# Lightweight convolution and a two-layer silu block on Trainium2: the first blocks' taps in PSUM, an earlier halo, and a new order of the steady block

## The chip, the cores and the metric

The kernel runs on one core of one Trainium2 chip. The metric is the device time of one execution in microseconds (us). A core has five engines that run side by side, each with its own stream of instructions: PE (TensorE, matrix products), DVE (VectorE), ACT (ScalarE), POOL (GpSimd) and SP (SyncE, which here issues most DMA transfers). Matrix products land in PSUM, eight banks of 128 partitions by 512 numbers; everything else lies in SBUF. Instructions wait for each other through semaphores.

## The reference

```python
def _attn_ref(x, weight):                       # x 8 x 4096 x 192, weight 8 x 7
    w = softmax(weight, axis=-1)                # over the 7 taps of each head
    x_pad = concat([zeros(8, 6, 192), x], axis=1)
    out[b, s, c] = sum_i w[c // 24, i] * x_pad[b, s + i, c]
...
def _moe_ref(x, w_in, w_out):                   # x 32768 x 192, 192 x 2048, 2048 x 192
    h = x @ w_in
    g = h * (1.0 / (1.0 + np.exp(-h)))
    return (g @ w_out).astype(np.float32)
```

So each channel is smoothed over seven positions in time (with six zeros ahead of each of the 8 sequences), then each of the 32768 tokens goes up from 192 to 2048 numbers, through silu, and down to 192. Everything is fp32.

## The kernel before

**Blocks.** The tokens are cut into 32 blocks of 1024. A block has two halves of 512 tokens, one in partitions 0 to 63 and one in 64 to 127, and the 192 channels are three thirds of 64. Block b goes through these stages; the letters are the tokens by which the order names them.

- `ld` loads the block (SP, L156) into a buffer `nat`. `i` turns it over with VectorE's 32x32 transposes (L490) into `xt`, channels in partitions. `ha` (halo_in, L502) puts the last six columns of the block before into the first six columns of `xt`: a copy from a small tile `tail` (on ScalarE, L509, for the blocks 1 and 2, on GpSimd, L511, for later ones; at the start of a sequence GpSimd writes zeros), then an SP DMA for the other half (L512).
- `v.ki` (conv, L515) is tap i of third k. Tap 0 is a scaled copy by ScalarE into `nat` (L521). Taps 1 to 6 have two forms. For blocks 1 and 2 VectorE multiplies and adds in one instruction (L529, `nat<-xt,taps,nat`). For later blocks ScalarE writes a scaled copy to a buffer u (L524), and a GpSimd DMA adds it into `nat` (L525, 18 per block).
- `sp` (spread) copies `nat` with SP DMAs (L546) into `dup`, where each half block has all its channels on either half of the partitions. `w.0` to `w.5` (win) are sums of parts of `dup` on VectorE (L563 and L566). w.0 and w.1 take `dup` in, w.2 to w.5 build on these.
- The up product is made in five groups g. A group has 15 products `Pr.g` (L658, TensorE, two run side by side on the two halves of the rows of the array) where the plain way has 18: the sums of inputs (w) and of weights allow it. `u`, `X`, `a`, `b` add up the results: u is a copy by ScalarE out of PSUM into a u buffer (L707), X, a and b are sums on VectorE (L701), and `S` is silu on ScalarE (L719). A small rest goes through plain products `L` (L675) and `SL`.
- `t1` to `t13` are sums of silu's results (L783, VectorE): t1 to t4 over 128x2048 numbers in parts `tC` and `tD` of 128x1024 each, the others whole.
- The down product has 20 products `Qr.j` for each of four j (L794, TensorE, two side by side on the two halves of the columns) in place of 24. `O`, `C`, `d` are copies out of PSUM by ScalarE (L829, L831), `m` are sums on VectorE (L842), `o` transposes (L850), `st` the stores by SP (L857).

P8.2 is thus product 8 of group 2, and Q4.3 out product 4 with j = 3.

**Weights.** In the first 170 us the weights are loaded, rounded, and their sums are made on GpSimd (`combine`, `combine_out` with its list OUT_SUMS; in the profile these stand at L138, with `ws`, `wr`, `wall` and `wx` as outputs). Block 0 takes the plain way meanwhile: plain up products, 48 down steps (the tokens `dp`), then copies `cp`, transposes `op` (L897) and stores `stp` (L906).

**The order is written by hand.** Every instruction is pinned to its place in the program, and each engine runs its own instructions in that order. `START` is a list of tokens that is run once, `PLAN` one that is run once for each b. A token's first character gives its block:

```python
    BACK = {"-": 1, "=": 2, "+": -1, "~": 3, "*": -2}
...
    for t in START.split():
        step(2, t)
    for b in range(1, NB + 4):
        for t in plan:
            step(b, t)
```

So in one pass of PLAN, `-P8.2` belongs to block b-1, `w.0` to block b, `+v.12` to block b+1, `*ld.0` to block b+2 and `=st.3` to block b-2; a token whose block does not exist, or that has been done, is passed over. In START a bare token is block 2, `-` block 1, `=` block 0 and `+` block 3. The assignments CHAIN_BANKS, XBANKS, PLAIN_BANKS and OUT_BANKS say which PSUM bank each result lies in.

Of the kernel before, what the change touches and what calls it, by code (L numbers as in the profile page):

```python
# [11 lines left out]
AF = mybir.ActivationFunctionType  # L12
ALU = mybir.AluOpType
# [4 lines left out]
def kernel(  # L18
# [24 lines left out]
    nc = tc.nc  # L43
# [3 lines left out]
    H, K = weight.shape  # L47
# [30 lines left out]


    PLAN = (  # L80
# [24 lines left out]
    )  # L105
    START = (
# [9 lines left out]
    )  # L116
    QUEUE = (0, 4, 1, 2, 3)
    CHAIN_BANKS = (
        (5, 7, 2, 5, 3),
        (4, 3, 1, 4, 6),  # L120
        (0, 6, 0, 6, 0),
    )
    XBANKS = {
        2: (1, 6, 3, 6, 0),
        4: (2, 1, 7, 0, 2),
    }
    PLAIN_BANKS = (7, 2, 0)
    OUT_BANKS = {"DX": 0, "DY": 2, "D2": 1, "D3": 4, "DC": 2}

    def pin(ins):  # L130
        return tc.keep_in_program_order(ins)
# [61 lines left out]
    for k in range(NK):  # L193
        rows_k = hot[SQ * k : SQ * k + SQ]
        for sign, base in ((1, 0), (-1, grp - 1)):
            pool.affine_select(
                out=rows_k,
# [8 lines left out]
    for e in range(2):  # L206
        half = one_hot[R * e : R * e + R].rearrange("p (a c) -> p a c", a=2)
        pool.affine_select(
            out=half,
# [133 lines left out]
    def combine(g, e):  # L343
# [40 lines left out]
        (("o", 1), ("o", 1), "+", ("o", 4)),  # L384
        (("o", 4), ("o", 4), "+", ("o", 10)),
        (("x", 1), ("o", 11), "+", ("o", 4)),
        (("x", 2), ("o", 5), "+", ("x", 1)),
        (("x", 1), ("o", 8), "-", ("x", 1)),
        (("x", 3), ("o", 0), "-", ("x", 1)),
        (("o", 10), ("o", 9), "-", ("o", 10)),  # L390
        (("o", 9), ("o", 9), "-", ("x", 3)),
        (("o", 4), ("o", 4), "n", ("o", 4)),
        (("o", 11), ("o", 11), "+", ("o", 9)),
        (("x", 4), ("o", 8), "-", ("o", 11)),
        (("o", 5), ("o", 5), "+", ("o", 8)),
        (("o", 3), ("o", 0), "+", ("o", 3)),
        (("o", 8), ("o", 1), "-", ("o", 8)),
        (("x", 7), ("o", 2), "+", ("x", 1)),
        (("o", 2), ("o", 2), "+", ("o", 8)),
        (("o", 0), ("o", 0), "+", ("o", 7)),  # L400
        (("x", 5), ("o", 6), "+", ("x", 4)),
        (("o", 6), ("o", 6), "-", ("o", 0)),
        (("x", 6), ("o", 3), "-", ("x", 4)),
        (("o", 7), ("o", 7), "n", ("o", 7)),
        (("o", 10), ("o", 11), "-", ("o", 10)),
        (("x", 0), ("x", 0), "n", ("x", 0)),
    )
    OUT_FORMS = {
# [88 lines left out]
    def tail_of(b):  # L497
        if (b + 1) * TT % S:
            tails[b + 1] = xpool.tile([R, NK, pad], F32, tag="tail", name="tail", bufs=2)
            pin(nc.sync.dma_start(out=tails[b + 1], in_=xts[b][R:P, :, TB : TB + pad]))  # L500

    def halo_in(b, _):  # L502
        xt = xts[b]
        if b * TT % S == 0:
            nc.gpsimd.memset(xt[0:R, :, 0:pad], 0.0)
        else:
            head = xt[0:R, :, 0:pad]
            if b <= 2:
                pin(nc.scalar.copy(head, tails.pop(b)))  # L509
            else:  # L510
                pin(nc.gpsimd.tensor_copy(head, tails.pop(b)))  # L511
        pin(nc.sync.dma_start(out=xt[R:P, :, 0:pad], in_=xt[0:R, :, TB : TB + pad]))  # L512
        tail_of(b)

    def conv(b, k, i):  # L515

        src = xts[b][:, k, i : i + TB]
        dst = nats[b][:, k, :, :].rearrange("p k c -> p (k c)")
        tap = taps[:, k, i : i + 1]
        if i == 0:  # L520
            pin(nc.scalar.activation(dst, src, AF.Copy, scale=tap))  # L521
        elif b > 2:
            z = free.pop(0)
            pin(nc.scalar.activation(z, src, AF.Copy, scale=tap))  # L524
            pin(nc.gpsimd.dma_start(out=dst, in_=z, accum_op=ALU.add))  # L525
            free.append(z)
        else:
            pin(
                nc.vector.scalar_tensor_tensor(  # L529
                    out=dst, in0=src, scalar=tap, in1=dst, op0=ALU.mult, op1=ALU.add  # L530
                )
            )

# [48 lines left out]
    def rows(t, e):  # L582
        return t[R * e : R * e + R]
# [29 lines left out]
    cmbs, banks = {}, []  # L613
# [24 lines left out]
    def plain_bank(b, i):  # L638
        return banks[PLAIN_BANKS[i]]

# [144 lines left out]
    def out_bank(node):  # L785
        name, e = OUT_HOME[node]
        return rows(banks[OUT_BANKS[name]], e)

# [15 lines left out]
    def mid(i):  # L804
        if not mids:
            cmb = xpool.tile([P, 4, TB], F32, tag="cmb", name="cmb")
            mids.extend(cmb[:, c, :] for c in range(4))
            mids.extend(xpool.tile([P, TB], F32, tag="yx", name="yx", bufs=2) for _ in range(2))
            mids.append(xpool.tile([P, TB], F32, tag="m4", name="m4"))
        return mids[i]  # L810
# [22 lines left out]
    def out_sum(b, i):  # L833
# [4 lines left out]
            lambda: (out_bank("Y"), rows(mid(2), 1)),  # L838
            lambda: (banks[OUT_BANKS["D3"]], mid(1)),
            lambda: (banks[OUT_BANKS["D2"]], mid(0)),  # L840
        )[i]()
# [162 lines left out]
    for j in (1, 2):  # L1004
        load_in(j, nc.sync)
    turn_in(0, 2)
    conv(0, 2, 0)
    for n in range(2):
        act.copy(dups[0][:, n, 0, :], by_pe[0][n])
    for i in range(1, K):  # L1010
        conv(0, 2, i)
    src = nats[0][:, 2, :, :].rearrange("p k c -> p (k c)")
# [87 lines left out]
```

## Time and profile before

| | us |
|---|---|
| time before, median of 3 runs (2344.7 to 2345.49) | 2345.25 |
| the profiled execution | 2346.1 |
| its span, first to last instruction | 2344.4 |
| its mean granted TensorE clock | 0.993 |
| first out products of block 1 | 167.04 |
| 30 periods from there, first out product to first out product | to 2294.64 |
| VectorE's taps, one instruction (L529) | 0.752 to 0.95 |
| a sum in SBUF (L563); with an operand in PSUM (L701) | 0.69; 0.68 to 0.70 |

The span cut in 40 equal slices, one digit a slice: TensorE's busy tenths, those of GpSimd, and the tenths of full speed at which TensorE's clock was granted.

```profile
PE   9879999999999999999999999999999999999997
...
POOL 5932222122222122222122222122221222221100
PEclk9989999999999999999999999999999999999999
```

The second and third slices (59 to 176 us) are where TensorE is less than full, and where GpSimd is busiest. In the lists below, a line of waits reads: engine, output and line, the engine, tile and line it waited for, then us in total, times, longest. A line of the timeline reads: start, length (both in us from the start of the span), engine, line, operation, output and inputs, partitions x elements, and how many instructions in a row (xN); in brackets the idle time before the first of them and what ended it. SPq and POOLq are the DMA issues of SP and GpSimd. PE shows an instruction of a row of like ones: where two products run side by side, each is counted.

### The profile page before, as it was taken

What the parts mean: (1) busy time and instruction counts of PE and PEld (TensorE: products, weight loads), DVE (VectorE), ACT (ScalarE), POOL (GpSimd) and SP (SyncE); (2) the same over time, 40 slices, a digit from 0 to 9 for tenths busy, and PEclk for the clock granted to TensorE, in tenths of its full rate; (3) what the DMA queues carried; (4) which work ended last, traced back from release to release, by engine and by line L of the source; (5) the groups of instructions that cost most, each with busy time, mean ns of one, the idle gap of its engine ahead of it and who ended that gap; (6) DMA issues with size and microseconds to landing.
All of it is one profiled execution on the core that took longest, in us unless ns stands there. A gap on an engine that the chain in (4) does not pass through costs nothing.

```text
span 2344.4 us, 31919 instructions
## 1 busy us (share of the span) xinstructions
PE 2304.3 (98%) x10622; PEld 994.2 (42%) x10622; DVE 2060.9 (88%) x2302; ACT 1562.5 (67%) x2835; POOL 552.8 (24%) x698
## 2 busy tenths in 40 slices
PE   9879999999999999999999999999999999999997
PEld 5234344444344443444443444443444444444433
DVE  8858899888889888899888998888998889998887
ACT  6266667776667766667766677766677766677643
POOL 5932222122222122222122222122221222221100
PEclk9989999999999999999999999999999999999999
DMA  7345667656666556676556676556676566665401
GB/s 164 67 74 90 116 114 126 107 100 101 115 115 119 102 101 113 109 122 115 98 99 115 111 124 111 102 96 118 116 124 106 100 101 115 115 119 94 75 13 18
DMA packets 526276, 242.66 MB, mean 104 GB/s; under 512 B 431840, under 2 KB 436960, under 8 KB 526112
## 3 DMA queue, kind: packets, MB, share of 16 engines
q0 software_dynamic: 75616, 138.45, 34.8%
q1 hardware_dynamic: 449440, 102.04, 24.8%
q8 instruction: 84, 1.38, 0.3%
q14 instruction: 80, 0.66, 0.1%
q10 hardware_dynamic: 1056, 0.13, 0.0%
HBM read 31.46 MB, written 25.17 MB: 24 GB/s over the span
## 4 chain that ended last, share of the span: by engine, by line
PE 92%; POOL 4%; DMA 1%; SPq 1%; DVE 1%; issue 1%; ACT 0%; DVEq 0%; POOLq 0%; ACTq 0%
PE ps L794 45%; PE ps L658 44%; PE ps L675 2%; POOL ws L138 2%; POOL wr L138 2%; DMA dup<-nat 1%; POOL wall L138 0%; DMA ws<-wr 0%; POOL wx L138 0%; DVE win L563 0%; DMA g<-in_moe_w_in_dram 0%; SPq L156 0%; SPq L546 0%; SPq L249 0%; SPq L254 0%
## 5 line engine op out<-in xcount | busy, mean ns | idle before, releaser
L525 POOL DMA_DIRECT2D nat<-u x522 | 444.6, 883 | 1604.5 <-ACT u L524 1090.1
L794 PE MATMUL ps<-g,wall 128*64 128x512 f32 x1984 | 774.3, 594 | 0.4 <-DVE g L701 0.4
L658 PE MATMUL ps<-win,wr 64*128 64x512 f32 x1550 | 674.2, 599 | 11.9 <-ACT u L707 8.7
L658 PE MATMUL ps<-win,ws 64*128 64x512 f32 x1550 | 604.5, 597 | 0.0
L707 ACT COPY u<-ps 128x512 f32<-128x512 f32 x775 | 445.1, 588 | 103.7 <-PE ps L658 97.7
L794 PE MATMUL ps<-g,wx 128*64 128x512 f32 x1240 | 424.8, 592 | 0.0
L658 PE MATMUL ps<-dup,wr 64*128 64x512 f32 x868 | 398.0, 592 | 0.1
L794 PE MATMUL ps<-t,wall 128*64 128x512 f32 x992 | 391.1, 595 | 0.0
L794 PEld LDWEIGHTS ps<-g,wall 128*64 128x64 f32 x1984 | 224.0, 137 | 347.2 <-issue 323.7
L524 ACT ACTIVATE u<-xt,taps 128x512 f32<-128x512 f32 x522 | 359.5, 722 | 1.4
L701 DVE TENSOR_TENSOR g<-u,ps 128x512 f32<-128x512 f32 x465 | 313.9, 680 | 38.6 <-PE ps L658 28.2
L658 PEld LDWEIGHTS ps<-win,wr 64*128 64x128 f32 x1550 | 258.8, 187 | 167.2 <-issue 100.2
L658 PEld LDWEIGHTS ps<-win,ws 64*128 64x128 f32 x1550 | 241.0, 187 | 192.4 <-issue 136.9
L658 PE MATMUL ps<-dup,ws 64*128 64x512 f32 x682 | 304.2, 595 | 14.4 <-DVE ps L701 14.4
L719 ACT ACTIVATE g<-ps 128x512 f32<-128x512 f32 x465 | 269.2, 603 | 70.5 <-PE ps L658 70.5
L719 ACT ACTIVATE g<-g 128x512 f32<-128x512 f32 x465 | 277.4, 634 | 42.8 <-DVE g L701 42.8
L783 DVE TENSOR_TENSOR t<-g 128x1024 f32<-128x1024 f32 (+1 forms) x217 | 292.2, 1369 | 4.2 <-ACT g L719 0.7
L794 PE MATMUL ps<-t,wx 128*64 128x512 f32 x744 | 288.1, 594 | 0.0
L701 DVE TENSOR_TENSOR ps<-u,ps 128x512 f32<-128x512 f32 x310 | 212.8, 695 | 52.6 <-PE ps L658 44.8
L794 PEld LDWEIGHTS ps<-g,wx 128*64 128x64 f32 x1240 | 130.5, 137 | 222.6 <-issue 222.3
L829 ACT COPY cmb<-ps 64x512 f32<-64x512 f32 x124 | 72.0, 581 | 213.5 <-PE ps L794 213.5
L783 DVE TENSOR_TENSOR t<-g,t 128x2048 f32<-128x2048 f32 x93 | 210.0, 2285 | 1.1
(99 smaller groups left out, 2397.8 us busy)
## 6 DMA issues: line engine op xcount, KB each, us to landing
nat<-u POOLq DMA_DIRECT2D x522, 256.0 KB, 4.0
dup<-nat SPq DMA_DIRECT2D x345, 128.0 KB, 2.4
nat<-in_x_dram SPq DMA_DIRECT2D x382, 64.0 KB, 3.7
out_dram<-yx SPq DMA_DIRECT2D x248, 64.0 KB, 2.0
out_dram<-cmb SPq DMA_DIRECT2D x124, 64.0 KB, 2.0
raw<-in_moe_w_out_dram SPq DMA_DIRECT2D x8, 384.0 KB, 4.1
g<-in_moe_w_in_dram SPq DMA_DIRECT2D x8, 192.0 KB, 5.8
ws<-wr POOLq DMA_DIRECT2D x8, 192.0 KB, 5.9
```

Source lines behind the costliest of these rows:

```text
L138: return lambda *args, **kw: pin(getattr(self.engine, name)(*args, **kw))
L524: pin(nc.scalar.activation(z, src, AF.Copy, scale=tap))
L525: pin(nc.gpsimd.dma_start(out=dst, in_=z, accum_op=ALU.add))
L658: nc.tensor.matmul(to[:, cols], raw(g, *LEFT[e][r], e), rhs[:, cols], start=first, stop=True, skip_group_check=True,)
L675: nc.tensor.matmul(plain_bank(b, n and 1 + e)[:, cols], rows(wr[j] if own == e else ws[j], e)[:, a, k, :], rows(dups[b], e)[:, SLOT[e][2 * ...
L701: pin(nc.vector.tensor_tensor(out_, u, v, op=op))
L707: pin(nc.scalar.copy(us[b, g, o][:, cols], t1[:, cols]))
L719: pin(nc.scalar.activation(h, src, AF.Silu))
L783: pin(engine.tensor_tensor(g_part(to, js), g_part(u, js), g_part(v, js), op=op))
L794: nc.tensor.matmul(out_bank(node), out_form(OUT_FORMS[r])[:, j, :], g_part(OPERAND[r], j), start=first, stop=True, skip_group_check=True,)
L829: pin(nc.scalar.copy(to(), out_bank(node)))
```

## The change

1. *Taps of blocks 1 and 2.* The partial sums of their taps are kept in three PSUM banks (one for each third) instead of `nat`; only the last tap of a third writes `nat`.
2. *Halo.* ScalarE instead of GpSimd copies the halo of block 3 also. Block 4 begins a sequence, so GpSimd's copies begin with block 5.
3. *START.* w.3, w.4 and w.5 of block 1 stand right behind w.2, ahead of most of block 2's taps; they stood behind all of these.
4. *t1.* Its two VectorE sums of 128x1024 (tC1, tD1) become one sum by GpSimd over 128x1536 (tA1) and one by VectorE over 128x512 (tB1).
5. *PLAN* has a new order throughout, with other PSUM banks. Twenty-five weight sums of OUT_SUMS are the same ones in another order.

The number of matrix products and their operands' sizes stay. The line numbers of the new kernel are 10 higher than those given here from L546 on down, up to 5 higher a little above.

```diff
+++ halo_in, conv
-            if b <= 2:
+            if b <= 3:
                 pin(nc.scalar.copy(head, tails.pop(b)))
...
+    CONV_BANKS = (2, 3, 4)
+    taken = {}
...
+        taken[b, k] = taken.get((b, k), 0) + 1
+        acc = banks[CONV_BANKS[k]] if b in (1, 2) else dst
         if i == 0:
-            pin(nc.scalar.activation(dst, src, AF.Copy, scale=tap))
+            pin(nc.scalar.activation(acc, src, AF.Copy, scale=tap))
...
                 nc.vector.scalar_tensor_tensor(
-                    out=dst, in0=src, scalar=tap, in1=dst, op0=ALU.mult, op1=ALU.add
+                    out=dst if taken[b, k] == K else acc,
+                    in0=src,
+                    scalar=tap,
+                    in1=acc,
+                    op0=ALU.mult,
+                    op1=ALU.add,
+++ START
-        "-w.0 -w.1 =dp.35 =dp.36 v.00 =dp.37 =dp.38 -w.2 =dp.39 =dp.40 =dp.41 v.01 =dp.42 v.20 "
-        "=dp.43 =dp.44 v.02 v.03 v.10 v.11 v.12 v.13 v.14 v.15 v.16 v.04 v.05 v.06 v.22 v.23 "
-        "v.24 v.25 v.26 =dp.45 =cp.0 =dp.46 =dp.47 =cp.1 v.21 -w.3 =cp.2 -w.4 -w.5 =op.0 =op.1 "
+        "-w.0 -w.1 =dp.35 =dp.36 v.00 =dp.37 =dp.38 -w.2 -w.3 -w.4 -w.5 =dp.39 =dp.40 =dp.41 "
+        "v.01 =dp.42 v.20 =dp.43 =dp.44 v.02 v.03 v.10 v.11 v.12 v.13 v.14 v.15 v.16 v.04 v.05 "
+        "v.06 v.22 v.23 v.24 v.25 v.26 =dp.45 =cp.0 =dp.46 =dp.47 =cp.1 v.21 =cp.2 =op.0 =op.1 "
+++ PLAN: its beginning, then the steps around the turn from up to out products
-        "=Q10.1 =Q7.2 =Q6.0 =Q10.2 =Q10.0 =Q8.2 =Q10.3 =Q8.0 -w.2 +i.0 =Q8.1 =Q1.1 =d.b =d.B "
-        "=Q1.2 =Q7.1 =Q8.3 -w.3 =Q2.2 -w.5 +i.2 =Q2.0 =m.1 =Q19.0 -X2.4 =m.0 +ha.0 =m.4 =Q2.3 "
-        "=Q7.0 -w.4 -P13.4 -u2.0 =m.5 =m.3 =m.2 -SL.0 +v.10 -P1.4 -P9.4 +v.20 -P1.0 -P5.1 "
...
-        "-P6.2 -b5.1 -X2.3 -u2.2 -S5.1 -b5.0 -P1.3 -a0.1 -P9.3 -X4.3 -P13.3 -P14.1 -P1.2 -S2.3 "
-        "-P3.2 -tD1 -u0.3 -P7.3 -P11.3 -u0.2 -P0.3 -P12.3 -S5.0 -X2.2 -S3.1 -P9.2 -P0.2 -a5.3 "
-        "-u1.3 -S4.3 -P13.2 -P4.3 -u1.2 -tC2 -X4.2 -P14.3 -P12.2 -b1.3 -P14.2 -P7.2 =o.2 -S2.2 "
-        "sp.0 -b1.2 -P11.2 -P10.3 -P10.2 -a1.3 P5.4 -a5.2 -S1.0 sp.2 -P8.3 -S0.1 +v.22 -tC3 "
-        "-S3.3 P5.0 -P4.2 -S4.2 -S3.2 -b5.2 +v.01 -b5.3 u5.4 +v.14 +v.26 -S5.2 -S5.3 L.00 "
-        "-Q17.0 -Q4.2 -Q17.2 -a0.3 u5.0 -Q4.1 -S1.1 -Q17.1 w.0 -Q4.0 w.1 -tD2 -a1.2 -Q4.3 "
-        "-Q17.3 P2.0 P3.4 -S0.3 -O.0 -tD3 -S1.3 P2.4 -C.0 -S1.2 -S0.0 u4.4 -P8.2 -tC4 -Q12.1 "
+        "=Q14.1 =t13 +i.2 =Q14.0 +i.0 =Q1.2 +ha.0 =Q19.0 -w.4 =Q1.0 =Q10.2 -u2.0 =Q19.3 =d.A "
+        "=Q8.3 =Q10.1 =Q8.2 =Q10.3 =Q7.1 =Q10.0 =Q7.3 =Q2.0 =Q8.0 =Q2.2 =Q2.3 =d.B =d.b -u2.4 "
+        "=m.4 =Q8.1 -X2.4 =m.3 -P3.0 -P1.0 -P1.4 =m.5 -X2.0 -P13.4 -P9.4 -P5.1 -u0.0 -P13.0 "
+        "-P0.0 =m.1 -S2.4 -u0.4 +v.20 -P0.4 =m.2 -P9.0 -P12.4 -X4.4 -u5.1 -S2.0 -P11.4 -u1.4 "
...
+        "-tB1 sp.1 -P8.0 -b5.0 -X4.1 -a0.0 -P2.2 -u1.1 -P12.1 -P3.3 -P6.3 -b1.1 -S1.4 -P11.1 "
+        "-tA1 -P7.1 -u2.3 -X2.3 -u4.2 -P10.1 -P14.1 -a5.1 -S4.1 -S5.0 -P6.2 -S3.1 -u2.2 -b5.1 "
+        "-P9.3 -X4.3 *ld.1 ~st.3 -P1.3 -P13.3 -P4.1 -P3.2 -S5.1 -u0.3 -P1.2 -S2.3 -u0.2 -X2.2 "
+        "-a1.1 -P7.3 -P11.3 -P12.3 -P0.3 +v.12 -P9.2 -a5.3 -tC2 -P0.2 -P13.2 -P4.3 -S4.3 +v.24 "
+        "-u1.3 -P8.1 -S2.2 -P14.3 -X4.2 -b1.3 -u1.2 -P7.2 -P14.2 -a0.1 -a5.2 -a1.3 -P12.2 "
+        "-P11.2 -P10.3 -S1.1 -b1.2 -S3.3 -P4.2 -P8.3 -S1.3 -S0.1 -b5.3 -P10.2 P5.4 sp.0 -S1.0 "
+        "-S3.2 sp.2 -a1.2 P5.0 -a0.3 -S5.3 -b5.2 -P8.2 -Q4.3 -S1.2 +v.04 -Q17.1 -Q17.3 -Q4.2 "
+        "-a0.2 +v.15 -S5.2 -S4.2 -Q4.1 u5.0 -Q17.2 -tC4 w.0 u5.4 -Q4.0 -Q17.0 -O.0 L.00 w.1 "
+        "-C.0 P2.4 -tC3 -tD2 P2.0 P3.4 +v.23 +v.02 u4.0 u4.4 -S0.2 -Q5.1 -Q16.3 -Q3.2 -Q16.0 "
...
+++ banks
-    CHAIN_BANKS = ((5, 7, 2, 5, 3), (4, 3, 1, 4, 6), (0, 6, 0, 6, 0))
+    CHAIN_BANKS = ((5, 4, 2, 3, 3), (7, 5, 0, 1, 6), (0, 6, 4, 7, 2))
-    XBANKS = {2: (1, 6, 3, 6, 0), 4: (2, 1, 7, 0, 2)}
+    XBANKS = {2: (1, 1, 4, 7, 0), 4: (1, 0, 6, 6, 0)}
-    PLAIN_BANKS = (7, 2, 0)
-    OUT_BANKS = {"DX": 0, "DY": 2, "D2": 1, "D3": 4, "DC": 2}
+    PLAIN_BANKS = (0, 0, 2)
+    OUT_BANKS = {"DX": 7, "DY": 2, "D2": 1, "D3": 4, "DC": 2}
```

Steps of `tA` and `tB` exist in the kernel before too, unused: tA is GpSimd over the first three of four quarters of a sum, tB VectorE over the last.

More of the change, by code (lines that the diff above doesn't have):

```diff
@@ L118 @@
     CHAIN_BANKS = (
-        (5, 7, 2, 5, 3),
-        (4, 3, 1, 4, 6),
-        (0, 6, 0, 6, 0),
+        (5, 4, 2, 3, 3),
+        (7, 5, 0, 1, 6),
+        (0, 6, 4, 7, 2),
     )
     XBANKS = {
-        2: (1, 6, 3, 6, 0),
-        4: (2, 1, 7, 0, 2),
-    }
-    PLAIN_BANKS = (7, 2, 0)
-    OUT_BANKS = {"DX": 0, "DY": 2, "D2": 1, "D3": 4, "DC": 2}
+        2: (1, 1, 4, 7, 0),
+        4: (1, 0, 6, 6, 0),
+    }
+    PLAIN_BANKS = (0, 0, 2)
+    OUT_BANKS = {"DX": 7, "DY": 2, "D2": 1, "D3": 4, "DC": 2}
     def pin(ins):
@@ L386 @@
         (("x", 1), ("o", 11), "+", ("o", 4)),
+        (("o", 4), ("o", 4), "n", ("o", 4)),
         (("x", 2), ("o", 5), "+", ("x", 1)),
@@ L391 @@
         (("o", 9), ("o", 9), "-", ("x", 3)),
-        (("o", 4), ("o", 4), "n", ("o", 4)),
         (("o", 11), ("o", 11), "+", ("o", 9)),
         (("x", 4), ("o", 8), "-", ("o", 11)),
-        (("o", 5), ("o", 5), "+", ("o", 8)),
         (("o", 3), ("o", 0), "+", ("o", 3)),
-        (("o", 8), ("o", 1), "-", ("o", 8)),
-        (("x", 7), ("o", 2), "+", ("x", 1)),
-        (("o", 2), ("o", 2), "+", ("o", 8)),
         (("o", 0), ("o", 0), "+", ("o", 7)),
@@ L402 @@
         (("o", 6), ("o", 6), "-", ("o", 0)),
-        (("x", 6), ("o", 3), "-", ("x", 4)),
+        (("o", 5), ("o", 5), "+", ("o", 8)),
+        (("x", 7), ("o", 2), "+", ("x", 1)),
+        (("o", 8), ("o", 1), "-", ("o", 8)),
+        (("o", 2), ("o", 2), "+", ("o", 8)),
         (("o", 7), ("o", 7), "n", ("o", 7)),
         (("o", 10), ("o", 11), "-", ("o", 10)),
+        (("x", 6), ("o", 3), "-", ("x", 4)),
         (("x", 0), ("x", 0), "n", ("x", 0)),
```

25 rows, old and new, of the table PLAN are left out of this document.

## The prediction

> **What bounds the kernel now.** First part 1 of the page, which gives busy time by engine, and the waits of TensorE.
>
> ```profile
> span 2344.4 us, 31919 instructions
> PE 2304.3 (98%) x10622; PEld 994.2 (42%) x10622; DVE 2060.9 (88%) x2302; ACT 1562.5 (67%) x2835; POOL 552.8 (24%) x698
> ```
>
> ```profile
> PE ps L658 <- DVE ps L701: 14.4, 1, 14.4
> PE ps L658 <- ACT u L707: 8.7, 3, 7.2
> ```
>
> TensorE bounds it, and its two long waits happen once each. The change leaves all 5311 matmuls in place (two records each), so it can only win time in which TensorE stands still or works unpaired. I therefore looked for that time stage by stage in the timeline: the start (up to 167.0, when the first out products run), 30 steady blocks (167.04 to 2294.64, mean period 70.92) and the tail.
>
> **The start.** The timeline by engine, around the two waits:
>
> ```profile
> 68.55 15.64 DVE L529 SCALAR_TENSOR_TENSOR nat<-xt,taps,nat 128x512 f32<-128x512 f32 x18
> ...
> 89.00 15.64 DVE L529 SCALAR_TENSOR_TENSOR nat<-xt,taps,nat 128x512 f32<-128x512 f32 x18
> ...
> 107.15 1.88 DVE L897 STREAM_TRANSPOSE osb<-cmb 128x512 f32<-128x512 f32 x3
> ...
> 120.90 1.30 DVE L490 STREAM_TRANSPOSE xt<-nat 128x512 f32<-128x512 f32 x2 [11.28 <-DMA nat<-in_x_dram]
> ...
> 122.12 0.67 DVE L701 TENSOR_TENSOR ps<-u,ps 128x512 f32<-128x512 f32 x1
> ...
> 107.87 6.70 SPq L906 DMA_DIRECT2D out_dram<-osb  x12
> ...
> 114.61 4.23 SPq L156 DMA_DIRECT2D nat<-in_x_dram  x8
> ...
> 131.29 0.20 POOL L511 COPY xt<-tail 64x18 f32<-64x18 f32 x1
> ...
> 131.52 1.95 ACT L521 ACTIVATE nat<-xt,taps 128x512 f32<-128x512 f32 x3 [22.03 <-POOL xt L511]
> ...
> 122.85 1.22 PE L658 MATMUL ps<-dup,ws 64*128 64x512 f32 x1 [14.45 <-DVE ps L701]
> ...
> 135.08 1.22 PE L658 MATMUL ps<-win,wr 64*128 64x512 f32 x1 [7.22 <-ACT u L707]
> ```
>
> The reader is to see two chains. The first: VectorE's 36 taps (blocks 1 and 2) push the transposes of L897 to 107.15; the stores wait for those, the loads of block 3 stand behind the stores on SP, the two transposes of block 3 stand on VectorE ahead of the sum (L701) that TensorE needs: it rests until 122.85. The second: the halo of block 3 is behind GpSimd's weight sums until 131.29, the taps on ScalarE wait for the halo, and the copies of u stand behind the taps: TensorE rests until 135.08. Behind each rest come about 4.4 and 6 us in which matmul records are 1.0 us instead of 0.59 (granted clock 0.82 in 101 to 167).
>
> *Taps in PSUM.* The trace has no such instruction. With all operands in SBUF and GpSimd idle it takes 0.752 (start to start 0.788); beside GpSimd's sums 0.87 start to start. A plain sum takes 0.692 from SBUF alone (L563) and 0.680 to 0.696 with PSUM (L701), so PSUM costs nothing there. I take 0.79. The bounds are 0.73 (a sum into PSUM, 0.696, and the 0.036 that follows a dependent one) and 0.95 (the slowest tap now).
> [...]
>
> *Window sums ahead of taps.* All six (0.85 each beside GpSimd) now stand before the second block's taps; nothing is added. VectorE's chain is 68.55 + 18 x 0.79 + 2.35 (84.19 to 86.53, transposes and landing of the spread) + 6 x 0.85 + 18 x 0.79 = 104.4, against 107.15. The 13.75 from there to 120.90 (transposes, 12 stores, 8 loads, landing) and the 1.95 to the restart stay: 120.1 instead of 122.85. At 0.73 it would be 118.0, at 0.95 as late as 125.8. Before it rests, TensorE now also runs P3.0, P1.0 and P1.4, which stand ahead of P13.4, the product that waits for the sum X2.4: 13 instead of 10 products done.
>
> *Halo on ScalarE* (blocks 1 to 3). The copy costs 0.2 and waits only for the taps of block 2. Behind it on ScalarE stand the copies u2.0 and u2.4; they are needed at about 110, and 104.4 is earlier. The second rest (7.2) goes, and with it the second slow stretch. Late next is the first tap of block 3 that goes through a GpSimd DMA, and a copy of u that takes the same buffer eleven instructions later, by count near 133.
> That DMA stands behind the weight sums. They take about 0.85 each beside the taps and 0.45 (0.53 start to start) once VectorE rests, at 110 to 112. If taps with one SBUF input leave GpSimd alone, 31 of the 36 us of taps and window sums shrink by 0.38 and the weight sums end near 120: no wait. If not, the DMA goes at 131.3, lands 4.0 later (nat<-u), and the copy waits up to 3. Beside L701, which reads one operand from PSUM, weight sums at 121.4 to 129.3 kept their 0.72; I take no wait and keep 3 for the range.
> [...]
>
> Sum: 73 full-size products remained at 122.85 and took 44.2 = 31.2 (0.4277 a product, two running side by side) + 7.2 + 5.8 slow. Now 70 remain: 120.1 + 29.9 + 2.5 (one slow stretch) + 0.5 = 153.0 against 167.0. I take **-13**; from -5 (slow taps, late GpSimd) to -17.
>
> **The steady block.** The timeline of one block:
>
> ```profile
> 1090.16 0.64 PE L794 MATMUL ps<-g,wall 128*64 128x512 f32 x1
> ...
> 1093.75 0.69 PE L658 MATMUL ps<-win,wr 64*128 64x512 f32 x1
> ...
> 1094.71 1.47 PE L658 MATMUL ps<-win,wr 64*128 64x512 f32 x4
> ...
> 1096.11 0.64 PE L794 MATMUL ps<-t,wx 128*64 128x512 f32 x1
> ...
> 1091.85 0.69 DVE L563 TENSOR_TENSOR win<-dup 128x512 f32<-128x512 f32 x1 [0.92 <-DMA dup<-nat]
> ...
> 1092.58 0.69 DVE L563 TENSOR_TENSOR win<-win,dup 128x512 f32<-128x512 f32 x1
> ...
> 1093.19 1.22 DVE L783 TENSOR_TENSOR g<-g,t 128x1024 f32<-128x1024 f32 x1
> ...
> 1094.33 0.68 DVE L701 TENSOR_TENSOR g<-u,ps 128x512 f32<-128x512 f32 x1
> ```
>
> One pass runs 8 out products, 4 up products, 28 out, 4 up, 44 out, 76 up (six of them half-size). By the starts of these stretches they take 3.59, 2.36, 12.17, 1.92, 19.03 and 31.69. The two stretches of four are equal but for 0.44: in the first, the last product (P8.2) starts at 1095.06, 0.35 late, behind a1.2 (L701 at 1094.33), which stands behind w.0, w.1 and tD2; w.0 had waited for the spread. Without stalls a pass is 70.31; 0.61 x 30 = 18 is all there is to win.
>
> Written out as slots, the new order has stretches of 8, 4, 16, 4, 56 and 76: as many switches between up and out, and every pair again takes both halves of the array. So 70.31 stays the floor. The rest are places where TensorE needs a result just made; T is the start of the 8 out products.
> - P8.2 is now in the last up pair, at T - 1.00. The old 0.44 goes. Late next is a1.2 again: P4.2 starts at T - 2.71, is done 1.02 later, a1.2 takes 0.05 + 0.68, a further 0.05 to TensorE: T - 0.91. Cost 0.09, and more if VectorE is behind.
> - P2.4 (needs w.1) is due at T + 3.62. a0.2 follows P8.2 at T + 0.07, tC4 at 0.67, w.0 at 1.81, w.1 ends at 3.23: 0.34 to spare. The spread allows w.0 at T + 1.69 as now.
> - t1: VectorE does a quarter (0.69) instead of two steps of 1.21. GpSimd's 128x1536 is not in the trace; 64x128 takes 0.45 and 128x256 0.72, so 3.4 by extension, at most 6 beside two-input steps. It starts about 1.5 after P7.1 and tC2 needs it 6.3 later. Behind it on GpSimd stands v.12, needed a block later. Cost 0.
> - PSUM banks and the order of the weight sums change which buffer is waited for, not the number of steps; I found no other place with under 0.15 to spare but one, and one such place exists now.
>
> Per pass -0.44 + 0.09 + 0.07 for such places = -0.28, times 30: **-8.5**. Bounds: -15 (nothing late) and +6 (0.6 late in each).
>
> **The tail.** From the last matmul (2332.9) to the end there are three sums, three transposes, 12 stores. The new order leaves four sums (m.3, m.5, m.1, m.2, 0.6 each) behind Q8.1: **+0.5**, from -1 to +2.
>
> **Sum.** -13 - 8.5 + 0.5 = -21. The profiled execution took 2346.1 (span 2344.4 and 1.7 around it), 0.85 over the median of the runs shown, 2345.25; the terms are differences, so I set them against the median: 2324, and round to 2325.
>
> **Rivals.**
> - *GpSimd or the taps stay slow at the start*: -5 there, the rest as forecast: 2332. Against it stands 0.72 beside L701. Chance 0.15.
> - *The tight up places eat the steady gain*: the period stays at 70.9, -13 remains: 2333. For it: VectorE ran from 1086.74 to 1090.9 without a gap, where the new order asks for a1.2 at once. Chance 0.13.
> - *Nothing visible*: the first rest stays because the loads still stand behind the stores, and the steady block gives back 0.3 a pass: 2345 within 0.2%. Chance 0.07.
> - *Slower*: P8.2 behind a1.2, in every block. P4.2 and P8.2 were 5.9 apart by slots and are now 1.71; a backlog of VectorE at that point goes into TensorE one to one. It decides from about 0.9 a pass: 30 x 0.87 = 26 cancels the start's -13 and the -13 of the vanished 0.44. A backlog of one t sum (1.2) costs 30 x 1.2 = 36, so -13 - 13 + 36 + 0.5 = +10.5, about 2356. Against it: VectorE has 1.7 us less per block, and two adds before a1.2 wait for TensorE themselves. Chance 0.09.
> - The forecast has 0.56.
>
> About 0.2% (4.7 us) is what a measurement of this kernel can tell from no change. Faster by more than that 0.84, within it 0.07, slower 0.09. The range 2311 to 2340 takes in both partial cases and the bounds of taps and places.
>
> **What would show it.** Right: one long rest of TensorE ending near 120, no wait of ScalarE on the halo, weight sums at 0.45 to 0.55 beside the taps, first out products near 153, both stretches of four at 1.92, a mean period near 70.65. Wrong: taps over 0.87, a u copy waiting for nat<-u near 133, the stretch of 76 over 32, or w.0 waiting for the spread beyond T + 2.1.

## The result, and the profile after

The changed kernel takes 2315.24 us, median of 3 runs (2314.82 to 2315.82), against 2345.25: 30.0 us less, a ratio of 0.9873 with the interval 0.985 to 0.9895. The profiled execution took 2315.8 (span 2314.1). The forecast was 2325, in a range of 2311 to 2340. First the page of the changed kernel, part 1, then its waits of TensorE.

```profile
span 2314.1 us, 31693 instructions
PE 2288.6 (99%) x10622; PEld 922.3 (40%) x10622; DVE 2009.3 (87%) x2271; ACT 1550.2 (67%) x2836; POOL 652.4 (28%) x728
```

```profile
PE ps L668 <- DVE ps L711: 7.4, 1, 7.4
PE ps L668 <- ACT u L717: 2.8, 3, 1.3
```

The long wait for a VectorE sum is 7.4 instead of 14.4, and the 7.2 for a copy of u is gone (the three that are left are 1.3 at most). GpSimd is 100 us busier: t1 (31 x 3.54 = 110) less, in the main, what its weight sums gained. The difference of the two spans, 30.3, by stages (all from the starts of TensorE's stretches in the timelines of the two profiled executions):

| stage | before | after | difference | forecast |
|---|---|---|---|---|
| to the first out products | 167.04 | 153.79 | -13.25 | -13 |
| 30 periods | 30 x 70.92 | 30 x 70.344 | -17.3 | -8.5 |
| from there to the last matmul's start | 37.27 | 37.02 | -0.25 | (in the tail) |
| last matmul's start to the end | 12.48 | 12.97 | +0.5 | +0.5 |

**The start**, in the timeline of the changed kernel:

```profile
69.08 7.60 DVE L534 SCALAR_TENSOR_TENSOR ps<-xt,taps,ps 128x512 f32<-128x512 f32 x10
...
103.75 1.89 DVE L907 STREAM_TRANSPOSE osb<-cmb 128x512 f32<-128x512 f32 x3
...
118.57 1.31 DVE L490 STREAM_TRANSPOSE xt<-nat 128x512 f32<-128x512 f32 x2 [12.34 <-DMA nat<-in_x_dram]
```

```profile
104.48 7.88 SPq L916 DMA_DIRECT2D out_dram<-osb  x12
112.40 4.24 SPq L156 DMA_DIRECT2D nat<-in_x_dram  x8
```

```profile
116.55 0.72 POOL L138 TENSOR_TENSOR wx<-zeros,wx 128x256 f32<-128x256 f32 x1
...
110.38 0.19 ACT L509 COPY xt<-tail 64x18 f32<-64x18 f32 x1
...
120.52 1.22 PE L668 MATMUL ps<-dup,ws 64*128 64x512 f32 x1 [7.43 <-DVE ps L711]
```

The reader is to see the first chain still whole, only earlier: taps, transposes of L907, twelve stores, eight loads, transposes of block 3, restart. The second chain is gone: GpSimd's last weight sum ends at 117.3 instead of 131.3, and the halo is copied at 110.4. What a rest costs beyond itself stands in the windows of the same trace (start to end in us, length, TensorE's busy time and instructions, granted clock, DMA share, GB/s):

```profile
112.00:120.50 8.50, 1.09 (x3) 0.70 0.53 83
120.50:124.00 3.50, 3.48 (x8) 0.50 0.37 76
124.00:130.00 6.00, 6.00 (x26) 0.86 0.00 0
130.00:153.00 23.00, 23.00 (x115) 1.00 0.42 81
```

Over 3.5 us behind the rest the granted clock is 0.50, over the next 6 us 0.86 on the mean, then 1.00.

**The steady block.** In this execution all thirty passes have one length, 70.34 or 70.35, where 69.93 to 72.22 were seen before. The mean lengths of the stretches:

| | 8 out | 4 up | out | 4 up | out | 76 up | sum |
|---|---|---|---|---|---|---|---|
| before | 3.70 | 2.40 | 12.17 | 1.92 | 19.03 | 31.69 | 70.92 |
| after | 3.58 | 1.92 | 7.02 | 1.92 | 24.18 | 31.72 | 70.34 |

The timeline of one turn from up to out products (T, the start of the 8 out products, is 1068.27):

```profile
1067.21 0.69 PE L668 MATMUL ps<-win,wr 64*128 64x512 f32 x1
...
1068.27 0.64 PE L804 MATMUL ps<-t,wall 128*64 128x512 f32 x1
```

```profile
1066.47 1.29 DVE L711 TENSOR_TENSOR g<-u,ps 128x512 f32<-128x512 f32 x2
...
1068.98 1.22 DVE L793 TENSOR_TENSOR t<-g 128x1024 f32<-128x1024 f32 x1
1070.11 0.68 DVE L573 TENSOR_TENSOR win<-dup 128x512 f32<-128x512 f32 x1
```

The first of the two L711 is a1.2; P8.2 begins at 1067.21, 0.05 behind its end, and is late by 0.07. tC4 starts at T + 0.71, w.0 at T + 1.85, and w.0 carries no bracket: here it waits for nothing, and in no pass of this execution by more than 0.07.

### The profile page after: what moved, and what is told of

The parts are those of the page before. It is cut to its first block, busy times and chain, and to the rows that moved or that the text cites. A ratio compares the mean times of both kernels' runs of the same rounds, so it can differ in the third digit from the quotient of the medians.

```text
span 2314.1 us, 31693 instructions
## 1 busy us (share of the span) xinstructions
PE 2288.6 (99%) x10622; PEld 922.3 (40%) x10622; DVE 2009.3 (87%) x2271; ACT 1550.2 (67%) x2836; POOL 652.4 (28%) x728
## 4 chain that ended last, share of the span: by engine, by line
PE 95%; DVE 3%; SPq 1%; ACT 0%; issue 0%; DMA 0%; DVEq 0%
PE ps L804 46%; PE ps L668 44%; PE ps L685 3%; DVE ps L534 1%; DVE two L138 1%; PE ps L994 1%; PE ps L609 0%; SPq L916 0%; DVE mh L138 0%; SPq L156 0%; PE ps L448 0%; DVE t L793 0%; DMA nat<-in_x_dram 0%; ACT g L138 0%; DVE nat L534 0%
## 5 line engine op out<-in xcount | busy, mean ns | idle before, releaser
L804 PE MATMUL ps<-g,wall 128*64 128x512 f32 x1984 | 743.1, 595 | 0.0
L668 PE MATMUL ps<-win,wr 64*128 64x512 f32 x1550 | 685.8, 598 | 2.4 <-ACT u L717 2.4
L668 PE MATMUL ps<-win,ws 64*128 64x512 f32 x1550 | 644.2, 593 | 0.4 <-ACT u L717 0.4
L804 PE MATMUL ps<-g,wx 128*64 128x512 f32 x1240 | 414.5, 592 | 0.0
L804 PE MATMUL ps<-t,wall 128*64 128x512 f32 x992 | 368.0, 594 | 0.5 <-DVE t L793 0.5
L711 DVE TENSOR_TENSOR g<-u,ps 128x512 f32<-128x512 f32 x465 | 309.7, 683 | 31.5 <-PE ps L668 29.2
L729 ACT ACTIVATE g<-ps 128x512 f32<-128x512 f32 x465 | 279.9, 602 | 39.6 <-PE ps L668 39.0
L668 PEld LDWEIGHTS ps<-win,ws 64*128 64x128 f32 x1550 | 257.1, 187 | 121.5 <-issue 94.5
L711 DVE TENSOR_TENSOR ps<-u,ps 128x512 f32<-128x512 f32 x310 | 214.9, 694 | 92.4 <-PE ps L668 33.1
L668 PE MATMUL ps<-dup,ws 64*128 64x512 f32 x682 | 271.2, 591 | 7.4 <-DVE ps L711 7.4
L804 PE MATMUL ps<-t,wx 128*64 128x512 f32 x744 | 267.0, 594 | 1.3 <-ACT ps L841 1.3
L793 DVE TENSOR_TENSOR t<-g 128x512 f32<-128x512 f32 (+1 forms) x186 | 240.9, 1309 | 5.0 <-DVE g L793 0.5
```

What stands on the lines that cost most here:

```text
L668: nc.tensor.matmul(to[:, cols], raw(g, *LEFT[e][r], e), rhs[:, cols], start=first, stop=True, skip_group_check=True,)
L711: pin(nc.vector.tensor_tensor(out_, u, v, op=op))
L729: pin(nc.scalar.activation(h, src, AF.Silu))
L793: pin(engine.tensor_tensor(g_part(to, js), g_part(u, js), g_part(v, js), op=op))
L804: nc.tensor.matmul(out_bank(node), out_form(OUT_FORMS[r])[:, j, :], g_part(OPERAND[r], j), start=first, stop=True, skip_group_check=True,)
```

## The experiments

Each kernel was timed beside the kernel before, whose median was 2344.1 to 2345.8 in the three groups of runs; the changed kernel is the 2315.24 above, from a group of its own, so a difference from it of under 1.7 says nothing. "First out" is the start of the first out products in the profiled execution, and the mean period is from there too.

| kernel | median | against 2315.24 | first out | mean period |
|---|---|---|---|---|
| 1 taps in SBUF | 2319.46 | +4.2 | 157.97 | 70.36 |
| 2 halo on GpSimd | 2315.15 | -0.1 | 152.73 | 70.36 |
| 3 both undone | 2321.39 | +6.2 | 161.96 | 70.34 |
| 4 loads first | 2305.47 | -9.8 | 143.45 | 70.34 |
| 5 start only | 2333.47 | +18.2 | 154.19 | 70.92 |
| 6 t1 on VectorE | 2325.83 | +10.6 | 153.64 | 70.70 |
| 7 one extra | 2329.15 | +13.9 | 153.36 | 70.80 |
| 8 w.0 first | 2319.21 | +4.0 | 153.97 | 70.49 |
| 9 sums late | 2315.41 | +0.2 | 153.24 | 70.35 |
| 10 w.0 first, taps moved | 2319.95 | +4.7 | 154.12 | 70.49 |
| 11 two extra | 2351.09 | +35.9 | 155.17 | 71.52 |
| 12 before, loads first | 2345.43 | +30.2 | 165.50 | 70.92 |

The theory of the start: taps in PSUM shorten VectorE's chain and free GpSimd, and with GpSimd free the halo's engine matters no more. The rival: the halo took the second rest away.

**1. Taps in SBUF.**

```diff
-        acc = banks[CONV_BANKS[k]] if b in (1, 2) else dst
+        acc = dst
```

> The changed kernel, except that the taps of blocks 1 and 2 keep their partial sums in SBUF, as before. Theory (taps in PSUM leave GpSimd's weight sums alone, and they leave VectorE alone): taps go from 0.78 to 0.87 start to start, VectorE's chain ends about 3 us later, TensorE restarts near 123.5 instead of 120.5, the weight sums end near 130 instead of 117.3; the halo is on ScalarE, so no second rest. Start +3 to +5, in all 2318 to 2320. [...]

2319.46. The 36 taps take 0.857 each (0.871 start to start) against 0.753 (0.763) in the changed kernel. GpSimd's 64x128 sums from 68.5 to 108 take 0.79 on the mean, against 0.49; the last weight sum ends at 130.8 instead of 117.3. TensorE restarts at 124.25, and there is no second rest. Timeline:

```profile
124.25 1.22 PE L668 MATMUL ps<-dup,ws 64*128 64x512 f32 x1 [11.63 <-DVE ps L711]
```

The theory's numbers held, but for a restart 0.75 later than its 123.5.

**2. Halo of block 3 on GpSimd.**

```diff
-            if b <= 3:
+            if b <= 2:
```

> The changed kernel, except that GpSimd copies the halo of block 3, as before. Theory: with taps in PSUM the weight sums end at 117.3, and the halo's SP DMA went only at 119.9, behind stores and loads, so the engine of the halo costs nothing any more: within 0.7 of 2315.2. Rival (the halo on ScalarE is what took the second rest away): it comes back with its slow stretch, +7 to +13, 2322 to 2328.

2315.15, no difference. GpSimd copies the halo at 117.14, before its SP DMA can go (119.29, behind stores and loads). Timeline:

```profile
117.14 0.19 POOL L511 COPY xt<-tail 64x18 f32<-64x18 f32 x1
...
119.29 0.60 SPq L512 DMA_DIRECT2D xt<-xt  x1
```

**3. Both undone.** The edits of 1 and 2 together.

> The changed kernel with both undone: taps in SBUF and the halo of block 3 on GpSimd. Theory: the halo waits for weight sums that end near 130, the copies of u behind it on ScalarE wait, a second rest of about 7 us returns with a slow stretch: +10 to +14, 2325 to 2329, far more than the sum of the two undone alone. Rival (the two parts add up independently): the sum of the two single changes.

2321.39 (the profiled execution was 2.6 longer). The second rest is back. Timeline:

```profile
131.84 0.19 POOL L511 COPY xt<-tail 64x18 f32<-64x18 f32 x1
...
133.31 0.69 PE L668 MATMUL ps<-win,wr 64*128 64x512 f32 x1 [3.01 <-ACT u L717]
```

So the halo on ScalarE is worth 1.9 (2321.39 less 2319.46) where the taps are in SBUF, and nothing where they are in PSUM. The rest is 3.0, not the 7 I expected: the theory had the direction, its size was too large, and +6.2 lies nearer to the rival's sum, +4.1, than to +10.

This run also shows that part of the start's gain belongs to the rest of the change, the new PLAN above all. With taps and halo both as before, the first out products come at 161.96, 5.1 ahead of the kernel before, and since the periods and the end are those of the changed kernel, the 2.6 of this execution lie ahead of them too. The second rest is 3.0 here and 7.22 there, and the three products more ahead of the first rest are worth 1.3 by the prediction's 0.4277 a product. What in the new order shortens the second rest was not traced.

**4. Loads of block 3 ahead of block 0's stores**, on the changed kernel.

```diff
-        "... =dp.33 =dp.34 +ld.1 "
+        "... =dp.33 =dp.34 +ld.1 +ld.2 +ld.0 "
```

> The changed kernel with one move in START: the loads of thirds 2 and 0 of block 3 stand right behind those of third 1, ahead of block 0's stores on SP. Theory (the one rest left, 7.4 us before 120.5, is stores, then loads, then landing, 13 us behind VectorE's taps): the transposes of block 3 run at 105.6 instead of 118.6, TensorE goes on near 109, the rest and the slow stretch behind it go: -8 to -12, 2303 to 2307. Rival (another wait is late next: GpSimd's weight sums end at 117.3, the taps of block 3 need GpSimd's DMAs and free u buffers): -0 to -4, 2311 to 2315.

2305.47, the fastest of all: 0.9832 of the kernel before (0.9817 to 0.9847). In its timeline block 3 is turned at once, and in its windows (line 2, columns as above) TensorE is full where it rested:

```profile
106.12 1.86 DVE L490 STREAM_TRANSPOSE xt<-nat 128x512 f32<-128x512 f32 x3
```

```profile
112.00:120.50 8.50, 8.50 (x39) 1.00 0.29 51
```

Of the 10.3 by which the first out products come earlier, 7.4 is the rest; most of the others is the clock, which is 1.00 here in each window from 104 to 143, where behind the changed kernel's rest it was 0.50 and 0.86: 3.5 x 0.50 + 6 x 0.14 = 2.6 by estimate.

**12. The same move on the kernel before.**

> The kernel before with nothing but the loads of thirds 2 and 0 of block 3 moved behind those of third 1, the move that was worth 9.8 on the changed kernel. Theory (there the halo waits for GpSimd's weight sums until 131, so the first rest goes and the second one grows to the same end, 135): 0 to -2.5 against the kernel before. Rival (the first rest of 14.4 goes by itself): -9 to -14.

2345.43 against 2345.83 in the same group (ratio 0.9999, 0.999 to 1.0008). The waits change places. Timeline:

```profile
111.79 1.22 PE L658 MATMUL ps<-dup,ws 64*128 64x512 f32 x1 [3.14 <-DVE ps L701]
...
134.39 1.22 PE L658 MATMUL ps<-win,wr 64*128 64x512 f32 x1 [17.11 <-ACT u L707]
```

The first rest falls from 14.45 to 3.14, the second grows from 7.22 to 17.11, and its end moves by 0.7. GpSimd copies the halo there at 130.61. In both kernels the second wait ends 3.8 behind that copy (135.08 and 131.29 before, 134.39 and 130.61 here), wherever TensorE stood ahead of it; with GpSimd freed first, the same edit is worth 9.8.

**9. w.3, w.4, w.5 behind the taps again**, on the changed kernel.

```diff
-        "-w.0 -w.1 =dp.35 =dp.36 v.00 =dp.37 =dp.38 -w.2 -w.3 -w.4 -w.5 =dp.39 ..."
+        "-w.0 -w.1 =dp.35 =dp.36 v.00 =dp.37 =dp.38 -w.2 =dp.39 ..."
...
-        "v.21 =cp.2 =op.0 =op.1 "
+        "v.21 -w.3 =cp.2 -w.4 -w.5 =op.0 =op.1 "
```

> The changed kernel with w.3, w.4 and w.5 of block 1 behind block 2's taps again, as before. Theory (VectorE's chain has the same instructions either way, so the stores, the loads and the restart at 120.5 stay; the products that need w.3 come at 107, after it): within 0.7 of 2315.2. Rival (these sums let TensorE do three products more ahead of its rest, 3 x 0.43): +1 to +3.

2315.41: taken back by itself, this part of the change costs nothing that can be seen.

**5. The start's changes on the kernel before**, with its PLAN, banks and t1.

> The kernel before with the three changes at the start alone: taps of blocks 1 and 2 in PSUM, the halo of block 3 on ScalarE, w.3 to w.5 ahead of the taps. PLAN, banks, OUT_SUMS and t1 stay. Theory (start and steady block add up): the steady period stays at 70.9 with its waits of w.0, the first out products come at 153.8 or, as the old order has three products fewer ahead of the rest (3 x 0.43), at 155: -12 to -13.3 against the kernel before. Rival (the new order's beginning is needed for the start too): first out products at 158 to 162, -5 to -9.

2333.47; 10.8 less than the kernel before in the same group, and by the profiled spans 12.9 less (2344.4 to 2331.5). The medians thus miss the theory's -12 to -13.3, and the spans lie in it. The first out products come at 154.19, and the mean period is 70.92 as before. Start and steady block add up. Within the start the parts don't: these edits bring 12.9 with the old PLAN, and undoing taps and halo under the new one costs 6.2 (run 3).

**7 and 11. One and two more VectorE instructions ahead of a1.2.**

```diff
+        elif name == "z":
+            vec.tensor_reduce(extra, wr[0].rearrange("p a k c -> p (a k c)")[:, 0:TB], axis=AX.X, op=ALU.max)
...
-        "-S3.2 sp.2 -a1.2 P5.0 ..."
+        "-S3.2 sp.2 -z.1 -a1.2 P5.0 ..."
```

(Eleven has `-z.1 -z.2`.)

> The changed kernel with one more VectorE instruction right ahead of a1.2 in every pass: a maximum over 128x512 numbers of the weights into one number a partition, which nothing uses; some 0.6 to 0.7 us. The trace has 0.13 of idle there, and P8.2 starts 0.07 late already. Theory (from that place a backlog of VectorE goes to TensorE one to one, as the slower rival on record has it): 0.45 to 0.6 a pass, period 70.8 to 70.95, 2329 to 2334. Rival (the place has more room than the trace suggests, so the slower case was never near): under 0.15 a pass, 2315 to 2320.

> The changed kernel with two of the extra VectorE instructions ahead of a1.2 instead of one. One made the period 70.80 instead of 70.34 for 0.60 start to start. Theory (one to one beyond 0.14): 71.40, 2345 to 2349, as slow as the kernel before. Rival (VectorE or TensorE make up for part of it elsewhere in the pass): below 71.2, under 2341.

2329.15 and 2351.09. One takes 0.592 start to start and lengthens the period by 0.455; two take 1.317 (0.714 and 0.603) and lengthen it by 1.176. Both differ by 0.14. Ahead of a1.2 the changed kernel has that much room: a1.2 starts 0.73 behind the instruction before it, where 0.60 would do. Timeline of 7:

```profile
1071.44 0.68 DVE L138 TENSOR_REDUCE extra<-wr 128x1 f32<-128x512 f32 x1
1072.04 1.28 DVE L712 TENSOR_TENSOR g<-u,ps 128x512 f32<-128x512 f32 x2
```

Beyond that room a backlog there goes into TensorE one to one. With two the new kernel is slower than the one before (ratio 1.0024, 1.0014 to 1.0034).

**6. t1 on VectorE again.**

```diff
-        "-tB1 sp.1 ..."
+        "-tD1 sp.1 ..."
-        "-tA1 -P7.1 ..."
+        "-P7.1 ..."
-        "... -u2.2 -b5.1 "
+        "... -u2.2 -b5.1 -tC1 "
```

> The changed kernel, except that t1 is two VectorE sums of 128x1024 again, the first part where tB1 stood, the second behind b5.1; GpSimd adds nothing. VectorE gets 1.67 us more a pass ahead of a1.2, where its gaps are 2.47 by the trace (0.71 + 0.19 + 0.19 + 0.97 + 0.28 + 0.13). Theory: the gaps take it up, period 70.34 to 70.45, 2314 to 2319. Rival (only GpSimd's share lets a1.2 run at once, so that P8.2 in its new place is late without it): 0.4 to 1.2 a pass, 2327 to 2352.

2325.83: +0.36 a pass. My theory fell. The cost is just under the rival's 0.4, but the rival's mechanism isn't what the trace shows either: two products in mid stretch are late, 9.6 and 4.8 ahead of T (1072.74), with records of 0.69 instead of 0.59, and P8.2, the third line, is not. Timeline:

```profile
1063.10 0.69 PE L668 MATMUL ps<-win,wr 64*128 64x512 f32 x1
...
1067.96 0.69 PE L668 MATMUL ps<-dup,ws 64*128 64x512 f32 x1
...
1071.79 0.59 PE L668 MATMUL ps<-win,wr 64*128 64x512 f32 x1
```

VectorE's gaps add up to more than the new work, but not in the places where it stands. This was one placement; another might cost less.

**8. w.0 ahead of tC4**, a probe for the landing of the spread.

```diff
-        "... -Q17.2 -tC4 w.0 u5.4 ..."
+        "... -Q17.2 w.0 -tC4 u5.4 ..."
```

> The changed kernel with w.0 one place earlier, ahead of tC4, so that it waits for the spread where it has to: a probe of when the spread lands. Before, w.0 ran at 1.69 (up to 3.15) behind the first out product of the pass and had waited 0.9 (up to 2.25) for the spread. Theory (the taps' accumulating DMAs of GpSimd have moved away from that stretch; in the 3 us behind the first out product they take 5% of the DMA engines instead of 59%, and the spread lands in 2.6 instead of 4.2 us): w.0 starts at 0.7 to 1.1, waits under 0.4 in most passes; period 70.3 to 70.4, 2313 to 2318. Rival (the spread lands as late as before, and w.0 is only placed behind its landing): w.0 at 1.7 after a wait of 1.0, and w.1 is late for P2.4 by some 0.9: 2330 to 2343, with longer waits every five passes.

2319.21, one above the theory's range. In 24 of 30 passes w.0 begins 0.71 to 1.02 behind T (in 22 of them at 0.71 to 0.75) and the pass keeps its 70.34. In six it begins at 1.16 to 2.58; these passes are longer by 0.12 to 1.53, in all 4.5. Each of the six comes five passes after the one before it. The timeline of one (T is 1070.59), and of the DMA queues from 3 us ahead of T to 3 us behind it the one that the profile labels instruction, queue 8 (packets, MB, share of the engines):

```profile
1072.19 0.69 DVE L573 TENSOR_TENSOR win<-dup 128x512 f32<-128x512 f32 x1 [0.81 <-DMA dup<-nat]
```

```profile
q8 instruction: 1, 0.02, 1.2%
```

Of the 30 such windows of this run seven held a transfer of queue 8: these six, and one in which it came 1.6 behind T, when w.0 had begun. In the kernel before, such a transfer stood in the windows of five passes, with w.0 at 2.14 or later (237.8, 592.4, 947.6, 1302.4, 1869.4); the only other was the last pass, where w.0 did not wait. A second instruction queue, 14, with 8 KB at a time, goes with less: in the eight windows of run 8 that held it alone, w.0 came at 0.71 to 1.02 and no pass was longer; in run 10 one such pass had w.0 at 1.28 and was 0.24 longer.

So there are two things: the spread lands earlier than before, and it is late, by 0.4 to 1.9 in run 8, where a transfer of queue 8 comes beside it. That these transfers cause the lateness was not tested. The changed order hides the second behind tC4: eight of its windows hold such a transfer, and no pass is longer. It does not hide all of it: in the profiles of runs 9, 1 and 2, which have the same PLAN, one pass each with such a transfer has w.0 at 2.11, 2.42 and 2.44 and is 0.06, 0.37 and 0.39 longer.

**10. The probe, with two taps moved back towards the spread.**

```diff
-        "-S3.2 sp.2 -a1.2 P5.0 -a0.3 -S5.3 -b5.2 -P8.2 -Q4.3 -S1.2 +v.04 -Q17.1 ..."
-        "-a0.2 +v.15 -S5.2 ..."
+        "-S3.2 sp.2 +v.04 +v.15 -a1.2 P5.0 -a0.3 -S5.3 -b5.2 -P8.2 -Q4.3 -S1.2 -Q17.1 ..."
+        "-a0.2 -S5.2 ..."
```

> The kernel with w.0 ahead of tC4 (2319.2), and two taps of a later block (v.04, v.15) moved from just behind the turn to the out products to 2 to 3 us ahead of it, so that their accumulating DMAs run while the spread runs, as in the kernel before. w.0 began 0.71 behind the first out product in most passes, and TensorE was late by what exceeds 1.04. Theory (these DMAs take the engines from the spread): w.0 begins at 1.0 to 1.8 in most passes, 0 to 0.7 a pass, 2321 to 2341, most likely near 2330. Rival (the spread lands early for another reason): w.0 stays at 0.71 in most passes, 2318 to 2321.

2319.95, w.0 at 0.71 to 0.78 in 22 passes, as in 8. But the test missed its stretch: the two DMAs were issued at T + 0.05 and T + 0.66 instead of T + 1.1 and T + 1.7, while the part of the spread that w.0 needs is issued at T - 2.3. In the kernel before, GpSimd issued such DMAs at T - 2.5 and T - 0.4. That they hold up the spread is still only argued (from T to T + 3 of one pass they take 58.7% of the DMA engines before and 5.0% after); the other causes weren't tried.

## Why the prediction was right, and where it was not

- **What bounds the kernel**: right. Every gain that was traced was time in which TensorE stood, or ran at the lowered clock behind a rest (0.50 over 4.4 us and 0.52 over 6.0 in the kernel before).
- **Taps in PSUM**: right. Forecast 0.79 start to start, measured 0.763; VectorE's chain ended at 103.8 (forecast 104.4), the restart came at 120.5 (forecast 120.1). The 13.75 in between, taken as it was, came to 14.7, since the twelve stores took 7.88 on SP instead of 6.70. PSUM costs a tap nothing that shows: 0.753 with it beside GpSimd's sums, 0.752 with SBUF alone and GpSimd idle (the six taps from 12.96 in the kernel before).
- **GpSimd's weight sums**: right, and with more effect than written: 0.49 on the mean from 68.5 to 108, the last at 117.3 (forecast near 120). In the traces a 64x128 sum takes 0.79 beside taps with two SBUF inputs (the kernel before, 68.5 to 108) and 0.45 beside taps with one (the changed kernel, 69 to 82.6; medians).
- **Halo on ScalarE**: right about the second rest, wrong about its cause. I wrote that this part takes the rest away. Run 2: it is worth nothing as soon as the taps are in PSUM, which bring GpSimd's sums to an end in time. And with neither part the rest is 3.0 and not 7.2 (run 3).
- **Window sums ahead of taps**: nothing to be seen, as the chain's count said (run 9).
- **Sum of the start**: -13 forecast, -13.25 measured. The closeness is in part luck: the terms as written add up to 153.0, which is -14.0, and the -13 takes one off without a reason. The first out products came at 153.79, 0.4 late from the restart and 0.4 from what follows it.
- **The steady block**: the step that failed, -8.5 for -17.3. Its terms: the old 0.44 (0.48 on the mean) went, 30 x 0.04 = 1.2 more than written. The added 0.09 + 0.07 came to 0.03 (76 up products 31.72 for 31.69): 30 x 0.13 = 3.9. P8.2 is late by 0.07, near the 0.09 worked out, but the stretch grows by less than half of that, and no other place cost anything. The remaining 3.6 (30 x 0.12) is w.0's late passes: in the kernel before, the 8 out products and the wait behind them take 3.58 or 3.59 in 25 passes and 3.71 to 4.71 in the five with a transfer of queue 8, 3.65 more in all. I had seen that w.0 waits for the spread and left those waits out of the sum, with "the spread allows w.0 at T + 1.69 as now". Run 8 shows it allows 0.71 in most passes, and that it is tC4 ahead of w.0 that hides the late ones: without it they cost 4.5. The measured -17.3 lies outside the term's own bounds, -15 to +6; the total lies in its range because that is wide. The room that P2.4 has behind w.1, worked out as 0.34, is 0.20: w.0 at 2.11 already costs 0.06 (run 9).
- **The signs**: the single rest, the halo, the weight sums, the first out products and both stretches of four came as written; the period did not, 70.34 for 70.65.
- **t1**: the estimate of GpSimd's 128x1536, 3.4, was good (3.54), and "cost 0" held. What I did not price is its gain: without it the period is 0.36 longer (run 6).
- **The tail**: +0.5 forecast; +0.5 behind the last matmul, -0.25 ahead of it.
- **Rivals**: the slower one had the right place and price (runs 7 and 11); the backlog of 1.2 that it needed wasn't there: 0.14 of room was left. "Nothing visible" is what run 12 shows, for a different edit of the kernel before.

## What to carry to other kernels

Where two waits follow each other closely, measure each part both alone and with the other in place: moving the loads gave nothing on the old kernel and 9.8 us on the new one, and the halo gave 1.9 or nothing. An accumulator with a short life can go to PSUM, and the engine that works beside it may gain more from that than the instruction itself (a tap 0.753 for 0.857, a 64x128 sum of GpSimd 0.49 for 0.79 on the mean, run 1). Put a result that comes by DMA behind independent work of the length of its worst lateness, not of its usual one; here tC4, 1.22 long, covers most of a lateness of 0.4 to 1.9, not all.

## What the runs showed of the hardware

- A VectorE tap with two SBUF inputs took 0.857 on the mean beside GpSimd's 64x128 sums and 0.752 with GpSimd idle; these sums took 0.79 beside such taps and 0.45 once they were over, at 107 to 113 (medians, the kernel before). With one input in PSUM the taps took 0.753 on the mean and the sums beside them 0.45 (the changed kernel).
- Transfers of queue 8, which the profile labels instruction, one of 16 KB in a window of 6 us, go with a spread that lands 0.4 to 1.9 us late (run 8), though they take only 0.9 to 1.7% of the DMA engines' time there (runs 8 and before).
- After a rest of 7.4 us (the changed kernel) TensorE's granted clock was 0.50 for the next 3.5 us and 0.86 on the mean of 6 more; where only waits of 1.3 or less were left (run 4), it was 1.00 from 104 us to 143.
